# A column for the constant: folding dc into VectorE's head sums in a two-layer linear-attention kernel

## The chip, the core and the metric

The kernel runs on one core of a Trainium2 chip. The metric is the device time of one execution in microseconds (us). Before the change the median of three runs is 866.07 us (866.04 to 866.49).

## The reference

The program is two identical layers, each of a linear-attention block and a GELU block, on x of 2048 rows by 448 columns in float32. With 16 heads of 28 columns the attention is:

```python
phi = lambda t: jnp.where(t > 0, t + 1, jnp.exp(t)) + 1e-6
pq, pk = phi(q), phi(k)                       # q, k, v = layernorm(x) @ wqkv
kv = einsum("bhsd,bhse->bhde", pk, v)
z = einsum("bhsd->bhd", pk)                   # sum of pk over all rows
num = einsum("bhqd,bhde->bhqe", pq, kv)
den = einsum("bhqd,bhd->bhq", pq, z)[..., None] + 1e-6
x = x + (num / den) @ wo
x = x + gelu(layernorm(x) @ w1 + b1) @ w2 + b2
```

The change concerns `den` alone. The kernel keeps e, which is phi without its 1e-6, so that den = sum over d of (e + 1e-6) z_d + 1e-6 = sum of e z_d, plus a constant per head, dc = 1e-6 times the sum of z_d, plus 1e-6.

## The kernel before, in words

The 2048 rows are 16 tiles of 128 rows, and four tiles make a block. A layer has two halves.

- **First half** (`phase1`): for each tile the layer norm, the projections to k and q, phi, and the product G of x with phi(k), summed over all tiles in four PSUM banks. Each float32 factor is split into a high and a low part, and three products stand for one. The phi(q) tiles are stored to DRAM.
- **Second half**: for each block, q over den times a matrix M (kv and wo folded together), the sum with x, a layer norm, and the GELU block `mlp1`, `mlp2`.

Between the halves lies a stretch of some 35 us in each layer, whose order is written out by hand in the table `ORDER` (L660 to L664). It is read token by token, and each engine's instructions stand in the order in which the tokens issue them. The tokens that the change and the prediction speak of are:

- `G`: the last tile's share of G on TensorE (L651). In the middle of it `trans_z` (L794) sums phi(k) over the partitions with a product with ones; ScalarE copies that to zb (L799), and VectorE sums zb by heads into dc (L802, a tile of 128x16).
- `gt`: G's four banks are copied to SBUF as gt, three by ScalarE (L809) and the fourth by VectorE (L811). Behind the first copy ScalarE turns dc into 1e-6 times dc plus 1e-6 (L814).
- `qz1 qz0 qz2 qz3`: for the four tiles of block 0 GpSimd multiplies phi(q) (the tile pq) by zb into the tile pz (`q_z`, L875).
- `qd0`: `q_den` for tile 0: VectorE sums pz by heads into dn (L880), adds dc (L881) and takes the reciprocal rd (L883). `qt0` multiplies pq by rd (L890). `qs1`, `qs2`, `qs3` are both for the other tiles.
- `Qx`, `Qu`, `Qy`: parts of a q projection put in as work for TensorE. `Qp`: phi of an earlier projection, three instructions on ScalarE (L631 to L633), a sum on GpSimd (L634) and a store.
- `kv`: TensorE makes kvp from gt and wv (L821, 32 instructions). `mask`: VectorE masks it into kvm (L825). `m0` to `m3`: TensorE multiplies kvm by wo (L831). `ms0` to `ms3`: ScalarE and VectorE split that into Mh (L843) and Ml (L844).
- `tq1`, `tq0`, `tq2`, `tq3`: TensorE transposes the scaled pq (L901). `qh`, `ql`: ScalarE and VectorE split the result (L908, L913). `o`: TensorE's product with M (L922 to L924). `la`, `lb`, `tu`, `st`, `sp`, `x`: layer norm, a turn through DRAM, and the splits (L347, L348) from which `mlp1` (L997) starts.

The tile pool hands out buffers in turn: a new tile waits until its buffer's last user is done. Before, pz of block 0 lay in three buffers, W5 for tiles 1 and 3, W4 for tile 0, and one of the two `xn` buffers for tile 2. `xn` also holds weights under way in layer 0 and later the normalised rows xm.

Of the kernel before, what the change touches and what calls it, by code (L numbers as in the profile page):

```python
# [11 lines left out]
AF = mybir.ActivationFunctionType  # L12
OP = mybir.AluOpType
# [9 lines left out]
def linear_attn_mlp_kernel(  # L23
# [12 lines left out]
    pe, act, dve, pool, sp = nc.tensor, nc.scalar, nc.vector, nc.gpsimd, nc.sync  # L36
    x0 = x_in[0]
    y_out = out[0]
    S, D = x0.shape
    F = w1.shape[1]  # L40
    H, DH = 16, 28
# [3 lines left out]
    G = 112  # L45
# [21 lines left out]
    def t448(tag, bufs, name, dt=F32):  # L67
        bufs = NH if tag == "H" else bufs
        return work.tile([128, D], dt, name=name, tag=tag, bufs=bufs)
# [3 lines left out]
    def t512(tag, bufs, name, dt=F32, at=0):  # L73
        n = 576 if tag in "BF" else 512
        return work.tile([128, n], dt, name=name, tag=tag, bufs=bufs)[:, at:at + 512]

    def f(ap):
        return ap.bitcast(F32)
# [100 lines left out]
    tiny = consts.tile([128, 1], F32, name="tiny")  # L179
# [3 lines left out]
    mask = consts.tile([G, G], F32, name="mask")  # L183
# [246 lines left out]
    def background(n, m=NF):  # L430

        for g in bg_wait[:m]:
            bg_wait.pop(0)()
        for _ in range(n):
            g = next(bg, None)
            if g is not None:
                bg_wait.append(g)
# [157 lines left out]
    def phi_min():  # L595
        l, t, o = qo.pop(0)
        e = t512("e" if t < NT - 2 else "E", 3 if t < NT - 2 else 2, "eq")[:, :D]
        dve.tensor_scalar(e, o, 0.0, None, op0=OP.min)
        begun.append((l, t, o, e))
# [37 lines left out]
    def stage_g(l, t, acc, mid=lambda: None):  # L637
# [20 lines left out]


    ORDER = [  # L660
# [3 lines left out]
    ] * LAYERS  # L664
# [139 lines left out]
    def trans_gt(tr, acc):  # L804
        tr.gt = []
        for c in range(4):
            s = t512("A" if c < 2 else "B", 2, "gt")[:, :D]
            if c < 3:
                act.copy(s, acc[c])  # L809
            else:  # L810
                dve.tensor_copy(s, acc[c])  # L811
            tr.gt.append(s)
            if c == 0:
                act.activation(tr.dc, tr.dc, AF.Identity, scale=1e-6, bias=tiny)  # L814

    def trans_kv(tr):
        tr.kvp = bank("m", 2, "kvp")[:G, :D]
# [16 lines left out]
    def trans_ms(tr, g):  # L834
        if g == 0:
            tr.Mh, tr.Ml = [], []
        if g % 2 == 0:
            for n in ("Mh", "Ml")[:1 if g else 2]:
                s = work.tile([128, 1024], F32R, name=n, tag="S", bufs=5)
                getattr(tr, n).extend(s[:G, i * D:(i + 1) * D] for i in range(2))  # L840
        if g >= 2:
            tr.Ml.append(t512("F", 2, "Ml", F32R)[:G, :D])
        act.copy(tr.Mh[g], tr.mp[g])  # L843
        dve.tensor_sub(tr.Ml[g], tr.mp[g], f(tr.Mh[g]))  # L844
# [20 lines left out]
    pqt, qs, pzs = {}, {}, {}  # L865

    def load_pq(l, b, j):
        t = b * 4 + j
        pqt[l, t] = t448(f"W{j}", 1, f"pq{l}_{t}")
        sp.dma_start(pqt[l, t], pq_d[l][t * 128:(t + 1) * 128, :])  # L870

    def q_z(l, b, j, tr):
        pz = t512("xn", 2, "pz")[:, :D] if (b, j) == (0, 2) else t448(f"W{4 if b else 4 + j % 2}", 1, "pz")
        pzs[l, b, j] = pz
        pool.tensor_tensor(pz, pqt[l, b * 4 + j], tr.zb, op=OP.mult)  # L875

    def q_den(l, b, j, tr):
        pz = pzs.pop((l, b, j))
        dn = consts.tile([128, H], F32, name="dn", tag="dn", bufs=1)
        dve.tensor_reduce(dn, pz.rearrange("p (h d) -> p h d", d=DH), axis=mybir.AxisListType.X, op=OP.add)  # L880
        dve.tensor_tensor(dn, dn, tr.dc, op=OP.add)  # L881
        rds[l, b, j] = work.tile([128, H], F32, name="rd", tag="rd", bufs=2)
        dve.reciprocal(rds[l, b, j], dn)  # L883

# [2 lines left out]
    def q_times(l, b, j):  # L887
        pq = pqt[l, b * 4 + j]
        p3 = pq.rearrange("p (h d) -> p h d", d=DH)
        dve.scalar_tensor_tensor(p3, p3, 1e-6, rds.pop((l, b, j))[:, :, None].to_broadcast([128, H, DH]),  # L890
                                 op0=OP.add, op1=OP.mult)

    def q_scale(l, b, j, tr):
        q_den(l, b, j, tr)
        q_times(l, b, j)
# [245 lines left out]
    for l in range(LAYERS):  # L1141
        tr = SimpleNamespace(mp={})
        za, acc = phase1(l, tr)
        if l == 0:
            background(0)
        fill = list(range(DEFER, NT))

        def biases(j):
            if l == 0:
                sp.dma_start(b1s, b1.rearrange("(c p) -> p c", p=128))  # L1150
                sp.dma_start(b2b, b2[None, :].to_broadcast([128, D]))

        def pre(j):
            for k in range(4):
                load_pq(l, 1, k)
            if l == 0:
                background(2)

        tok_ = SimpleNamespace(
            Q=lambda j: stage_q(l, fill.pop(0)), Qp=lambda j: fill_qphi(), Qv=lambda j: stage_qphi(j or 9),  # L1160
            Qi=lambda j: phi_first(), Qm=lambda j: phi_min(), Qe=lambda j: phi_exp(), Qj=lambda j: phi_last(), Qs=lambda j: store_phi(),
            Qx=lambda j: stage_q(l, fill[0], (0, 1)), Qu=lambda j: stage_q(l, fill[0], (2,)), Qy=lambda j: stage_q(l, fill.pop(0), (3,)),
            Qa=lambda j: stage_q(l, fill.pop(0), tag="acc"), G=lambda j: stage_g(l, NT - 1, acc, lambda: trans_z(tr, zs[l])),
            ld=lambda j: (load_pq(l, 0, j), load_x(l, j)), gt=lambda j: trans_gt(tr, acc),
            kv=lambda j: trans_kv(tr), mask=lambda j: trans_mask(tr), m=lambda j: trans_m(tr, j),
            ms=lambda j: trans_ms(tr, j), qz=lambda j: q_z(l, 0, j, tr), qs=lambda j: q_scale(l, 0, j, tr),
            qd=lambda j: q_den(l, 0, j, tr), qt=lambda j: q_times(l, 0, j),
            tq=lambda j: q_transpose(l, 0, j), qh=lambda j: q_high(l, 0, j), ql=lambda j: q_low(l, 0, j), o=lambda j: o_mm(l, 0, j, tr),
            la=lambda j: o_ln(l, 0, j), lb=lambda j: o_n(l, 0, j), x=lambda j: m_part(l, 0, j), tu=lambda j: turn_xm(l, j),
            st=lambda j: store_sq(("m", l, 0), j), sp=lambda j: spread(("m", l, 0), j),  # L1170
            sa=lambda j: spread(("m", l, 0), j, (sp, act)), pre=pre, b=biases)
        for tok in ORDER[l].split():
            name, j = tok.rstrip("0123456789"), int("0" + tok.lstrip("abcdefghijklmnopqrstuvwxyzQTG"))
            getattr(tok_, name)(j)
        assert not fill and not qo
        table(AF.Gelu_apprx_tanh)
        q_z(l, 1, 0, tr)
        mlp1(l, 0, 0)
        trans_chunks(tr)
        for b in range(NB):  # L1180
            acc = [bank("acc", 4, f"y{j}")[:, :D] for j in range(4)]
            nxt = b + 1 < NB
            if not nxt and l + 1 < LAYERS:
                st_k = stage_square(wqkv[:, D:2 * D])
                st_q = stage_square(wqkv[:, :D])
                load_to(l + 1, PRE - 1)
            for i in range(NF):
                if i + 1 < NF:
                    mlp1(l, b, i + 1)
                elif nxt:  # L1190
                    mlp1(l, b + 1, 0)
                if l == 0 and b == 0 and i:
                    background(1, 1)
                if i == NF - 2 and not nxt and l + 1 < LAYERS:
                    table(AF.Exp)
                if 9 <= i < 13:
                    add_bias(l, b, i - 9)
                if nxt:
                    behind(l, b, i, tr)
                elif l + 1 < LAYERS:  # L1200
                    if i == 2:
                        split_kq("k", st_k)
                    if i == 5:
                        split_kq("q", st_q)
                    if i in (3, 4, 6, 7, 8):
                        t = (3, 4, 6, 7, 8).index(i)
                        stage_a(l + 1, t)
                        stage_n(l + 1, t)
                        stage_t(l + 1, t)
                        if t % 2:  # L1210
                            stage_sp(l + 1, t)
                    if 9 <= i < 13:
                        stage_x(l + 1, i - 9)
                mlp2(l, b, i, acc)
# [28 lines left out]
```

## Time and profile before

| | |
|---|---|
| median of three runs | 866.07 us (866.04 to 866.49) |
| the profiled execution's own time | 865.61 us |
| its span in the trace | 863.5 us, 2.1 us less |
| TensorE's matmuls busy | 858.1 us, 99% of the span |
| VectorE / ScalarE / GpSimd busy | 495.4 / 350.5 / 210.3 us |
| the stretch between the halves, from the copy zb to the first mlp1 | layer 0: 101.4 to 134.1 us; layer 1: 526.0 to 559.2 us |

Times inside the trace are microseconds from the span's start. A row of the timeline gives the start, the duration, the engine (PE is TensorE's matmuls, PEld its weight loads, DVE is VectorE, ACT is ScalarE, POOL is GpSimd), the line, the operation, what it writes and reads, how many alike were merged, and in brackets the idle time of the engine before it and what ended that. An instruction that waits for a shared resource after its start shows a longer duration, not idle time.

### The profile page before, as it was taken

What the parts mean: (1) busy time and instruction counts of PE and PEld (TensorE: products, weight loads), DVE (VectorE), ACT (ScalarE), POOL (GpSimd) and SP (SyncE); (2) the same over time, 40 slices, a digit from 0 to 9 for tenths busy, and PEclk for the clock granted to TensorE, in tenths of its full rate; (3) what the DMA queues carried; (4) which work ended last, traced back from release to release, by engine and by line L of the source; (5) the groups of instructions that cost most, each with busy time, mean ns of one, the idle gap of its engine ahead of it and who ended that gap; (6) DMA issues with size and microseconds to landing.
All of it is one profiled execution on the core that took longest, in us unless ns stands there. A gap on an engine that the chain in (4) does not pass through costs nothing.

```text
span 863.5 us, 11706 instructions
## 1 busy us (share of the span) xinstructions
PE 858.1 (99%) x4157; PEld 768.4 (89%) x4157; DVE 495.4 (57%) x970; ACT 350.5 (41%) x624; POOL 210.3 (24%) x242
## 2 busy tenths in 40 slices
PE   9999999999999999999999999999999999999998
PEld 8999988888888888888899998988888888888887
DVE  7888686559456443236477877764664383533112
ACT  7676655323323322333356565533232233233231
POOL 3576612235013012012222343120320140140000
PEclk9999999999999999999999999999999999999999
DMA  5485646633313402051145442462332423111001
GB/s 171 152 275 171 207 109 214 194 113 123 120 64 123 137 1 98 1 182 49 49 156 186 160 129 96 143 206 82 121 112 81 140 74 110 49 50 43 1 1 43
DMA packets 68681, 97.89 MB, mean 113 GB/s; under 512 B 9488, under 2 KB 62864, under 8 KB 68624
## 3 DMA queue, kind: packets, MB, share of 16 engines
q1 hardware_dynamic: 67872, 96.76, 34.8%
q8 instruction: 32, 0.52, 0.3%
q10 hardware_dynamic: 752, 0.41, 0.2%
q14 instruction: 25, 0.20, 0.1%
HBM read 57.74 MB, written 36.18 MB: 109 GB/s over the span
## 4 chain that ended last, share of the span: by engine, by line
PE 98%; DVE 1%; issue 0%; ACT 0%; DVEq 0%
PE hp L997 32%; PE y L1027 10%; PE y L1026 10%; PE y L1028 10%; PE G L651 8%; PE psk L365 8%; PE psq L365 7%; PE op L934 2%; PE op L933 2%; PE op L935 2%; PE op L923 1%; PE op L922 1%; PE op L924 1%; PE mp L831 1%; PE op L937 1%; PE psk L579 1%
## 5 line engine op out<-in xcount | busy, mean ns | idle before, releaser
L1003 DVE TENSOR_TENSOR gl<-g,gh 128x512 fp32r<-128x512 f32 x112 | 83.2, 743 | 292.2 <-ACT gh L1002 292.2
L999 ACT ACTIVATE g<-hp,b1s 128x512 f32<-128x512 f32 x112 | 77.2, 689 | 400.6 <-PE hp L997 400.6
L1027 PE MATMUL y<-w2l,gh 128*128 128x448 f32 x447 | 163.6, 366 | 0.0
L1026 PE MATMUL y<-w2h,gh 128*128 128x448 f32 x447 | 162.0, 362 | 0.0
L1028 PE MATMUL y<-w2h,gl 128*128 128x448 f32 x447 | 160.0, 358 | 0.0
L997 PE MATMUL hp<-XH,w1h 128*128 128x512 f32 x336 | 130.7, 389 | 0.0
L997 PE MATMUL hp<-XH,w1l 128*128 128x512 f32 x336 | 130.7, 389 | 0.0
L997 PE MATMUL hp<-XL,w1h 128*128 128x512 f32 x336 | 130.1, 389 | 0.0
L215 POOL TENSOR_TENSOR brs<-bve,mhalf 128x1 f32<-128x1 f32 x55 | 34.6, 629 | 264.1 <-DVE bve L214 263.7
L1026 PEld LDWEIGHTS y<-w2h,gh 128*128 128x128 f32 x447 | 83.7, 187 | 9.4
L1027 PEld LDWEIGHTS y<-w2l,gh 128*128 128x128 f32 x447 | 83.9, 188 | 7.0
L1028 PEld LDWEIGHTS y<-w2h,gl 128*128 128x128 f32 x447 | 84.0, 188 | 5.0
L997 PEld LDWEIGHTS hp<-XL,w1h 128*128 128x128 f32 x336 | 63.1, 188 | 13.1
L997 PEld LDWEIGHTS hp<-XH,w1h 128*128 128x128 f32 x336 | 63.0, 187 | 10.7
L997 PEld LDWEIGHTS hp<-XH,w1l 128*128 128x128 f32 x336 | 63.1, 188 | 9.9
L1002 ACT CAST gh<-g 128x512 fp32r<-128x512 f32 x112 | 69.5, 621 | 3.6
L365 PE MATMUL psk<-wk,XH 128*128 128x448 f32 x210 | 61.8, 364 | 0.0
L875 POOL TENSOR_TENSOR pz<-pq,zb 128x448 f32<-128x448 f32 x32 | 37.4, 1176 | 96.4 <-DVE dn L880 62.1
L365 PE MATMUL psq<-wq,XH 128*128 128x448 f32 x196 | 57.1, 365 | 0.0
L490 POOL TENSOR_TENSOR xnl<-x,xnh 128x384 fp32r<-128x384 f32 x32 | 35.1, 1097 | 68.3 <-ACT xnh L489 55.0
L348 DVE TENSOR_TENSOR XL<-sp,XH 128x512 fp32r<-128x512 f32 x58 | 46.8, 818 | 5.5 <-ACT XH L347 5.5
L651 PE MATMUL G<-kh,xnh 128*128 128x448 f32 x128 | 46.7, 367 | 0.0
(185 smaller groups left out, 1490.9 us busy)
## 6 DMA issues: line engine op xcount, KB each, us to landing
x<-in_A_x_dram SPq DMA_DIRECT2D x32, 224.0 KB, 4.0
pq_d<-eq SPq DMA_DIRECT2D x32, 224.0 KB, 2.5
pq<-pq_d SPq DMA_DIRECT2D x32, 224.0 KB, 3.5
x<-x_d SPq DMA_DIRECT2D x32, 224.0 KB, 3.8
sq_a<-sq SPq DMA_DIRECT2D x13, 512.0 KB, 2.9
sp<-sq_a SPq DMA_DIRECT2D x52, 128.0 KB, 3.0
sq_q<-sq SPq DMA_DIRECT2D x12, 512.0 KB, 2.7
sp<-sq_q SPq DMA_DIRECT2D x48, 128.0 KB, 2.8
```

Source lines behind the costliest of these rows:

```text
L348: eng.tensor_tensor(lo.rearrange("p (c i n) -> p c i n", c=4, n=32), x, f(h), op=OP.subtract)
L365: pe.matmul(o, x, p, start=(i == 0), stop=(i == 10))
L490: pool.tensor_tensor(lo[:, :TL], xn[:, :TL], f(h[:, :TL]), op=OP.subtract)
L651: pe.matmul(acc[c], w, k, start=first and c not in others[0], stop=last and c not in others[1])
L875: pool.tensor_tensor(pz, pqt[l, b * 4 + j], tr.zb, op=OP.mult)
L997: pe.matmul(o, w, r, start=(k == 0), stop=(k == len(made) - 1))
L999: act.activation(g, hp, AF.Gelu_apprx_tanh, bias=b1s[:, i:i + 1])
L1002: act.copy(gh, g)
L1003: dve.tensor_sub(gl, g, f(gh))
L1026: pe.matmul(acc[j], gh[:, s], w2h[:, i], start=first, stop=False)
L1027: pe.matmul(acc[j], gh[:, s], w2l[:, i], start=False, stop=False)
L1028: pe.matmul(acc[j], gl[:, s], w2h[:, i], start=False, stop=stop)
```

## The change

pz of block 0 becomes a tile of 16 heads by 29 columns, 464 wide, always in one of the two `xn` buffers. GpSimd writes the products into columns 0 to 27 of each head (new L874). A new helper `times_tiny` has ScalarE write 1e-6 times dc plus 1e-6 into column 28 (new L882, token `dz`), and VectorE's sum runs over 29 columns (new L889), so that the add of dc disappears for block 0. Blocks 1 to 3 keep the add; for them the token `dc` turns dc as before, but later. In the order, the products of tiles 2 and 3 move behind `qs1` and `qd0`.

```diff
-  "Q ld1 ld0 ld2 ld3 G qz1 qz0 qz2 qz3 gt qs1 Qx Qp kv qd0 tq1 Qu mask qt0 qh1 ql1 m0 tq0 qs2 b ms0 qh0 m1 ms1 m2 "
+  "Q ld1 ld0 ld2 ld3 G qz1 qz0 gt dz1 dz0 qs1 qz2 dz2 Qx Qp kv qd0 qz3 dz3 dc tq1 Qu mask qt0 qh1 ql1 m0 tq0 qs2 b ms0 qh0 m1 ms1 m2 "
...
-            if c == 0:
-                act.activation(tr.dc, tr.dc, AF.Identity, scale=1e-6, bias=tiny)
...
-        pz = t512("xn", 2, "pz")[:, :D] if (b, j) == (0, 2) else t448(f"W{4 if b else 4 + j % 2}", 1, "pz")
-        pzs[l, b, j] = pz
-        pool.tensor_tensor(pz, pqt[l, b * 4 + j], tr.zb, op=OP.mult)
+        pq = pqt[l, b * 4 + j]
+        if b == 0:
+            pz = pzs[l, b, j] = t512("xn", 2, "pz")[:, :H * (DH + 1)].rearrange("p (h d) -> p h d", d=DH + 1)
+            pool.tensor_tensor(pz[:, :, :DH], pq.rearrange("p (h d) -> p h d", d=DH),
+                               tr.zb.rearrange("p (h d) -> p h d", d=DH), op=OP.mult)
+            return
+        pz = pzs[l, b, j] = t448("W4", 1, "pz")
+        pool.tensor_tensor(pz, pq, tr.zb, op=OP.mult)
+
+    def times_tiny(out, ds):
+
+        act.activation(out, ds, AF.Identity, scale=1e-6, bias=tiny)
...
-        dve.tensor_reduce(dn, pz.rearrange("p (h d) -> p h d", d=DH), axis=mybir.AxisListType.X, op=OP.add)
-        dve.tensor_tensor(dn, dn, tr.dc, op=OP.add)
+        if b:
+            pz = pz.rearrange("p (h d) -> p h d", d=DH)
+        dve.tensor_reduce(dn, pz, axis=mybir.AxisListType.X, op=OP.add)
+        if b:
+            dve.tensor_tensor(dn, dn, tr.dc, op=OP.add)
...
+            dz=lambda j: times_tiny(pzs[l, 0, j][:, :, DH], tr.dc), dc=lambda j: times_tiny(tr.dc, tr.dc),
```

VectorE's row in layer 0 from the fourth copy of G to the mask is shown first, before the change; dn is a tile's head sums, rd its reciprocal, and pq0_1, pq0_0 are the phi(q) of tiles 1 and 0.

```order
L811 COPY gt_1375<-G3_335 128x448
L880 TENSOR_REDUCE dn_1377<-pz_1360 128x16
L881 TENSOR_TENSOR dn_1377<-dn_1377,dc_1350 128x16
L883 RECIPROCAL rd_1380<-dn_1377 128x16
L890 SCALAR_TENSOR_TENSOR pq0_1_1326<-pq0_1_1326,rd_1380 128x448
L880 TENSOR_REDUCE dn_1414<-pz_1362 128x16
L881 TENSOR_TENSOR dn_1414<-dn_1414,dc_1350 128x16
L883 RECIPROCAL rd_1417<-dn_1414 128x16
L825 TENSOR_TENSOR kvm_1427<-kvp_1397,mask_121 112x448
L890 SCALAR_TENSOR_TENSOR pq0_0_1330<-pq0_0_1330,rd_1417 128x448
```

The same place of VectorE's row with the change:

```order
L811 COPY gt_1370<-G3_335 128x448
L889 TENSOR_REDUCE dn_1374<-pz_1360 128x16
L893 RECIPROCAL rd_1376<-dn_1374 128x16
L900 SCALAR_TENSOR_TENSOR pq0_1_1326<-pq0_1_1326,rd_1376 128x448
L889 TENSOR_REDUCE dn_1413<-pz_1362 128x16
L893 RECIPROCAL rd_1415<-dn_1413 128x16
L823 TENSOR_TENSOR kvm_1429<-kvp_1396,mask_121 112x448
L900 SCALAR_TENSOR_TENSOR pq0_0_1330<-pq0_0_1330,rd_1415 128x448
```

Two adds are gone ahead of the mask; two more go behind it, in front of the reciprocals of tiles 2 and 3.

ScalarE's row from the copy zb to the last instruction of `Qp`, before:

```order
L799 ACTIVATE zb_1348<-zp_1345,zc_119 128x448
L809 COPY gt_1368<-G0_332 128x448
L814 ACTIVATE dc_1350<-dc_1350,tiny_117 128x16
L809 COPY gt_1371<-G1_333 128x448
L809 COPY gt_1373<-G2_334 128x448
L631 ACTIVATE eq_1390<-psq_1314 128x448
L632 ACTIVATE ep_1391<-psq_1314 128x448
L633 ACTIVATE eq_1390<-eq_1390 128x448
```

And with the change, down to the split of tile 1:

```order
L799 ACTIVATE zb_1348<-zp_1345,zc_119 128x448
L809 COPY gt_1364<-G0_332 128x448
L809 COPY gt_1366<-G1_333 128x448
L809 COPY gt_1368<-G2_334 128x448
L882 ACTIVATE pz_1360<-dc_1350,tiny_117 128x16
L882 ACTIVATE pz_1362<-dc_1350,tiny_117 128x16
L882 ACTIVATE pz_1379<-dc_1350,tiny_117 128x16
L631 ACTIVATE eq_1389<-psq_1314 128x448
L632 ACTIVATE ep_1390<-psq_1314 128x448
L633 ACTIVATE eq_1389<-eq_1389 128x448
L882 ACTIVATE pz_1417<-dc_1350,tiny_117 128x16
L882 ACTIVATE dc_1350<-dc_1350,tiny_117 128x16
```

The copies of G's second and third bank have lost the instruction on dc ahead of them, and three writes of 128x16 stand ahead of `Qp`. The third, into pz_1379 (tile 2), lies in the buffer of pz_1360 (tile 1), so it waits for VectorE's sum of tile 1.

GpSimd's row, before:

```order
L875 TENSOR_TENSOR pz_1360<-pq0_1_1326,zb_1348 128x448
L875 TENSOR_TENSOR pz_1362<-pq0_0_1330,zb_1348 128x448
L875 TENSOR_TENSOR pz_1364<-pq0_2_1334,zb_1348 128x448
L875 TENSOR_TENSOR pz_1366<-pq0_3_1338,zb_1348 128x448
L634 TENSOR_TENSOR eq_1390<-ep_1391,eq_1390 128x448
```

And with the change:

```order
L874 TENSOR_TENSOR pz_1360<-pq0_1_1326,zb_1348 128x16x28
L874 TENSOR_TENSOR pz_1362<-pq0_0_1330,zb_1348 128x16x28
L874 TENSOR_TENSOR pz_1379<-pq0_2_1334,zb_1348 128x16x28
L634 TENSOR_TENSOR eq_1389<-ep_1390,eq_1389 128x448
L874 TENSOR_TENSOR pz_1417<-pq0_3_1338,zb_1348 128x16x28
```

The product of tile 3 has moved behind the sum of `Qp`, and waits for VectorE's sum of tile 0, whose buffer it takes. TensorE's and SyncE's rows are the same in both, apart from line numbers.

## The prediction

> **What bounds the kernel now.** I read the busy times first, then what TensorE waited for, then the timeline of the two stretches between the halves.
>
> ```profile
> PE 858.1 (99%) x4157; PEld 768.4 (89%) x4157; DVE 495.4 (57%) x970; ACT 350.5 (41%) x624; POOL 210.3 (24%) x242
> ```
>
> TensorE is the bound, and the change leaves its instructions alone. All that an edit elsewhere can win is TensorE's waiting. The view of waits has it complete:
>
> ```profile
> PE warm L170 <- DVE one L164: 1.1, 1, 1.1
> PE mp L831 <- DVE kvm L825: 0.5, 1, 0.5
> PE psk L579 <- ACT wk L137: 0.2, 1, 0.2
> ```
>
> Three waits, 1.8 us in all; two are in the launch, out of the change's reach. The one within it is of `m0` for the mask kvm. So nothing in the trace lets this change win more than about 0.7 us, and faster by 0.2% (1.7 us of 866.07; about what a measurement of this kernel can tell from no change) is out of reach. What it can lose has no such lid. The wait is in layer 1, and the timeline there (matmuls, VectorE, ScalarE, GpSimd) shows how it comes about:
>
> ```profile
> 526.25 0.37 PE L651 MATMUL G<-kh,xnl 128*128 128x448 f32 x1
> 526.57 0.53 ACT L809 COPY gt<-G 128x448 f32<-128x448 f32 x1
> 526.75 4.46 POOL L875 TENSOR_TENSOR pz<-pq,zb 128x448 f32<-128x448 f32 x4 [6.24 <-ACT zb L799]
> 526.86 0.36 PE L651 MATMUL G<-kh,xnl 128*128 128x448 f32 x1
> ...
> 527.36 0.31 ACT L814 ACTIVATE dc<-dc,tiny 128x16 f32<-128x16 f32 x1 [0.26 <-DVE dc L802]
> 527.71 0.97 ACT L809 COPY gt<-G 128x448 f32<-128x448 f32 x2
> ...
> 528.27 0.61 DVE L880 TENSOR_REDUCE dn<-pz 128x16 f32<-128x448 f32 x1
> 528.56 0.56 ACT L631 ACTIVATE eq<-psq 128x448 f32<-128x448 f32 x1
> 528.68 3.31 PE L821 MATMUL kvp<-gt,stg 128*112 128x112 f32 x32
> 528.98 1.17 DVE L881 TENSOR_TENSOR dn<-dn,dc 128x16 f32<-128x16 f32 x1
> 529.42 0.60 ACT L633 ACTIVATE eq<-eq 128x448 f32<-128x448 f32 x1
> 530.19 0.25 DVE L883 RECIPROCAL rd<-dn 128x16 f32<-128x16 f32 x1
> 530.47 1.22 DVE L890 SCALAR_TENSOR_TENSOR pq<-pq,rd 128x448 f32<-128x448 f32 x1
> 531.18 1.52 POOL L634 TENSOR_TENSOR eq<-ep,eq 128x448 f32<-128x448 f32 x1
> 531.62 0.61 DVE L880 TENSOR_REDUCE dn<-pz 128x16 f32<-128x448 f32 x1
> 532.26 0.47 DVE L881 TENSOR_TENSOR dn<-dn,dc 128x16 f32<-128x16 f32 x1
> 532.67 0.36 PE L372 MATMUL psq<-wq,XL 128*128 128x448 f32 x1
> 532.93 0.56 DVE L825 TENSOR_TENSOR kvm<-kvp,mask 112x448 f32<-112x448 f32 x1
> 533.41 0.61 DVE L890 SCALAR_TENSOR_TENSOR pq<-pq,rd 128x448 f32<-128x448 f32 x1
> 533.55 1.00 PE L831 MATMUL mp<-wot,kvm 112*112 112x448 f32 x2 [0.51 <-DVE kvm L825]
> 534.39 0.60 PE L901 MATMUL tq<-ident,pq 128*112 128x128 f32 x4
> ```
>
> kvp is done at 531.99, but VectorE reaches the mask only at 532.93. What holds it up are operations with two operands in SBUF that last as long as GpSimd works: the add takes 1.17 and 0.47 us, and the product with rd 1.22, where the same product takes 0.61 once GpSimd is idle. They end where a GpSimd instruction ends (four products from 526.75, 1.1 apiece, so one ends near 530.1, as does the first add). One side has the port, and the other stands still until it lets go. The sums (0.61) and the reciprocal (0.25) never stretch. Layer 0 has the same order with a luckier phase:
>
> ```profile
> 103.73 0.62 DVE L880 TENSOR_REDUCE dn<-pz 128x16 f32<-128x448 f32 x1
> ...
> 107.34 1.14 POOL L634 TENSOR_TENSOR eq<-ep,eq 128x448 f32<-128x448 f32 x1
> 107.61 0.56 DVE L825 TENSOR_TENSOR kvm<-kvp,mask 112x448 f32<-112x448 f32 x1
> ...
> 108.09 0.87 DVE L890 SCALAR_TENSOR_TENSOR pq<-pq,rd 128x448 f32<-128x448 f32 x1
> ```
>
> ```profile
> 108.23 0.27 PEld L831 LDWEIGHTS mp<-wot,kvm 112*112 112x112 f32 x2 [0.21 <-DVE kvm L825]
> 109.03 0.40 PEld L901 LDWEIGHTS tq<-ident,pq 128*112 128x112 f32 x4 [0.53 <-issue]
> ```
>
> There the mask is done at 108.17, the loads for `m0` follow at 108.23, and no matmul waits. But the load for `tq0` starts 0.07 after the scaled tile 0 (108.09 + 0.87 = 108.96): layer 0 has no slack at `tq0`.
>
> **The change, part by part.**
>
> *ScalarE before the sum.* The slot of dc (527.36 to 527.71, 0.35) leaves the front, so the second and third copies move up: at least by 0.35, at most to where their banks are ready (526.25 + 0.37 and 526.86 + 0.36, just after the first copy). The third then ends between 527.98 and 528.33 instead of 528.68, and the write for tile 1 (0.31, as dc's row) ends between 528.25 and 528.6. VectorE's sum now waits for it: it starts at 528.27 as before, or up to 0.33 later. I take the early end, since nothing else stands ahead of these copies. The 29th column makes the sum 464 elements instead of 448, 4% of 0.61, 0.02 us.
>
> *The two adds ahead of the mask* go: by their rows 1.17 and 0.47 in layer 1. The time does not fall by 1.64, since they were mostly waiting for GpSimd, and the next operation with two SBUF operands inherits that. So step by step in layer 1: sum of tile 1 to 528.88; reciprocal to about 529.2; GpSimd's product of tile 2, which now waits for that sum, starts at about 528.98, when tile 0's is done, and holds the port to 530.1; the product with rd then ends at about 530.6 (before: 531.69). Sum of tile 0 to 531.2, reciprocal to 531.4. Now kvp is the later one: mask from about 532.1 to 532.66. `m0` can follow the projection at 532.87 (532.67 and 0.20, the step of these matmuls) instead of 533.55: 0.68 earlier. The mask has 0.2 us to spare there, VectorE ahead of it 0.6.
>
> *What is late next: `tq0`.* It needs tile 0 scaled, behind the mask. On ScalarE the write for tile 2 waits for the sum of tile 1, with `Qp` queued behind it: write at 528.93, `Qp` from 529.28, and 1.46 later (528.56 to 530.02 before) it ends at 530.74. GpSimd's sum of `Qp` runs 530.8 to 531.9 and tile 3's product 531.9 to 533.0; VectorE's product for tile 0, issued at 532.6, gets the port at 533.0 and ends at 533.5. `tq0` comes 0.84 behind `m0` (533.55 to 534.39), at 533.71, and is not held up. Layer 1: **-0.68 us**; with the late end of the first item everything from the sum on is 0.33 later, tile 0 is ready at 533.84 and `tq0` goes at 533.95: -0.44.
>
> *The same in layer 0* gives: sum of tile 1 to 104.35, write for tile 2 at 104.4, `Qp` from 104.75 to 106.2, its sum on GpSimd 106.26 to 107.36, tile 3's product to 108.46, VectorE's product for tile 0 half a us behind that (before, GpSimd let go at 108.48 and the product ended at 108.96): 109.0. So `tq0` there stands where it stood, within 0.1; with the late end 0.35 later. Layer 0: **+0.05**, bounds -0.05 and +0.4. The earlier mask wins nothing there, since `tq0` sets the pace.
>
> *Off the path.* Of the adds of tiles 2 and 3 nothing is waited for. The writes for tile 3 and of dc stand on ScalarE between 531.3 and 532.0, where it waits for `tq1` anyway; the next user of dc is block 1. SyncE's queue has the same order: the store of `Qp` leaves its producer about a us earlier, and the biases behind it too.
>
> *GpSimd's products of 16 pieces.* The trace has no such product. Low end: as before, 1.1 us. For the high end two neighbours:
>
> ```profile
> 96.54 1.02 POOL L490 TENSOR_TENSOR xnl<-x,xnh 128x384 fp32r<-128x384 f32 x1
> 97.52 0.31 POOL L491 TENSOR_TENSOR xnh<-x,xnh 128x64 fp32r<-128x64 f32 x1
> ```
>
> 384 and 64 elements cost 1.02 and 0.31: 2.2 ns an element and 0.17 us an instruction (estimate). Were each head paid as an instruction, a product would cost 15 x 0.17 = 2.55 more, 3.6 us. I take 1.1: inputs are contiguous as before and only the write skips one column in 29. GPSIMD Engine Reference of the Trainium skill, § 7 "Performance pitfalls for Q7 kernels", has reads whose step is over 8 bytes at about half as much again per element; were this write, whose step inside a head is 4 bytes, charged so, an estimate of 1.65 a product would make the sum about +0.1 instead of -0.6. No row here shows such a step.
>
> *Does the gain last?* From `tq0` on, TensorE's own products feed the layer norm, the turn through DRAM and the splits, so these move with it:
>
> ```profile
> 557.07 1.20 ACT L347 CAST XH<-sp 128x512 fp32r<-128x512 f32 x2
> ...
> 559.16 0.39 PE L997 MATMUL hp<-XH,w1h 128*128 128x512 f32 x1
> ```
>
> The last high part is there 0.9 us before `mlp1` asks for it, and behind that the waits show none on which a gain could be lost. **Sum: -0.68 + 0.05 = -0.6 us**, bounds -0.75 and 0. On the profiled execution's own 865.61 (863.5 and 2.1 around it) that is 865.0; the runs' median lies 0.46 above it, so the forecast is 866.07 - 0.6 = **865.5**.
>
> **The rivals.**
>
> *The gain is given back at the port.* `tq0` in both layers hangs on who has the port when VectorE asks. With products of 1.2 to 1.9 us, or a sum that starts late, VectorE misses a turn in one layer or the other. Stepping the same chain with 1.2, 1.35, 1.65 and 1.9 a product gives -0.1, 0.0, +0.15 and +0.1 over both layers; a late sum alone 0.0. For it: layer 0 has 0.07 us of slack. Against: in layer 1 there is a wait of 0.68 to give away. Time about 866.1.
>
> *Slower: GpSimd pays for the pieces.* One mechanism: from some product length on, tile 3's product holds the port when VectorE comes to scale tile 2, and VectorE's Ml (L844) behind that is late for `o1`. At twice, 2.2 us: in layer 0 the products of tiles 1 and 0 end at 104.7 and 106.9, the mask ends at about 108.9, tile 0 is scaled at 110.15 (`tq0` +1.2), tile 3's product runs 111.2 to 113.4, tile 2 is scaled at 113.9 and `o1` waits another 0.6: +1.8. In layer 1 likewise +0.7. Together +2.5: 868.6. At 3.6 us it is about +14. The point is between 1.9 and 2.2 a product. For it: no strided write in the trace. Against: inputs contiguous, one instruction. The same page and section of the Trainium skill charges about 102 cycles for each read command that does not overlap the one before it; if the 16 heads were 16 commands, an estimate at that page's 1.2 GHz is 1.36 us more a product, 2.46, and +4.6 us. That is this rival's case; no row here shows it.
>
> *It does not do what it says:* the add's wait is taken over whole by the product behind it, and the mask stays late. Against: the mask can be 0.2 late before `m0` moves at all. 866.1, counted with the first rival.
>
> **How the numbers follow.** The forecast 57%, given back (or no effect) 27%, slower through GpSimd 13%, and 3% for a gain that the waits do not show. The first two are within 0.2%: 0.84 with rounding; slower 0.13; faster 0.03. The range holds the first two with the runs' spread (0.03 below to 0.42 above the median): 864.9 to 866.9.
>
> **What would show it.** In the changed profile: kvm no longer named in TensorE's waits in layer 1; VectorE's two sums and reciprocals without a stretched add; tile 3's product directly behind the sum of `Qp`, and VectorE's product for tile 0 stretched behind it; in layer 1 the step from kvp's end to `tq0` 1.7 us instead of 2.4 (531.99 to 534.39). The forecast is wrong if a product of GpSimd takes over 1.2 us, if `tq0` or `o` shows up among the waits, or if the sum of tile 1 waits for ScalarE.

## The result and the profile after

The changed kernel takes 864.65 us (median of 22 runs, 864.2 to 866.2), and before takes 866.23 us (22 runs, 865.07 to 868.23) in the same series. The ratio is 0.9985, with a 95% interval of 0.9978 to 0.9991, that is 0.8 to 1.9 us less. The difference is inside the 0.2% that the prediction called no change; its sign is the forecast one, and 864.65 lies 0.25 us below the low end of the stated range.

The profiled execution of the changed kernel happens to be one of its longer ones: 866.08 us, a span of 864.1 us, 0.6 more than the span of before. A comparison of the two spans would mislead. Stage by stage the traces say what happened. First, TensorE's busy time and the whole of its waits, after the change:

```profile
PE 859.2 (99%) x4157; PEld 768.3 (89%) x4157; DVE 493.6 (57%) x962; ACT 351.9 (41%) x632; POOL 210.9 (24%) x242
```

```profile
PE warm L170 <- DVE one L164: 1.1, 1, 1.1
PE psk L579 <- ACT wk L137: 0.3, 1, 0.3
```

The wait for the mask is gone; only the launch is left. To measure a stage independently of what came before it, I take two marks: the last matmul of the column sums, zp, and the first transpose of tile 0, `tq0`. The marks that the prediction doesn't show are, in before:

```profile
100.99 0.37 PE L797 MATMUL zp<-zl,ones 128*128 128x448 f32 x1
...
525.63 0.37 PE L797 MATMUL zp<-zl,ones 128*128 128x448 f32 x1
```

With `tq0` at 109.07 and 534.39, before takes 8.08 us in layer 0 and 8.76 in layer 1. The same stretch of layer 1 after the change, with all that TensorE, VectorE, ScalarE and GpSimd do on the path:

```profile
526.87 0.37 PE L797 MATMUL zp<-zl,ones 128*128 128x448 f32 x1
...
527.99 2.27 POOL L874 TENSOR_TENSOR pz<-pq,zb 128x448 f32<-128x448 f32 x2 [6.24 <-ACT zb L799]
528.95 0.97 ACT L809 COPY gt<-G 128x448 f32<-128x448 f32 x2 [0.61 <-PE G L651]
529.80 0.53 ACT L882 ACTIVATE pz<-dc,tiny 128x16 f32<-128x16 f32 x2
529.92 3.31 PE L819 MATMUL kvp<-gt,stg 128*112 128x112 f32 x32
530.24 0.64 DVE L889 TENSOR_REDUCE dn<-pz 128x16 f32<-128x464 f32 x1 [0.65 <-ACT pz L882]
530.95 1.14 POOL L874 TENSOR_TENSOR pz<-pq,zb 128x448 f32<-128x448 f32 x1 [0.69 <-DVE dn L889]
531.19 1.37 DVE L900 SCALAR_TENSOR_TENSOR pq<-pq,rd 128x448 f32<-128x448 f32 x1
532.49 0.62 DVE L889 TENSOR_REDUCE dn<-pz 128x16 f32<-128x464 f32 x1
532.62 1.15 POOL L634 TENSOR_TENSOR eq<-ep,eq 128x448 f32<-128x448 f32 x1 [0.53 <-ACT eq L633]
533.15 0.25 DVE L893 RECIPROCAL rd<-dn 128x16 f32<-128x16 f32 x1
533.32 0.57 DVE L823 TENSOR_TENSOR kvm<-kvp,mask 112x448 f32<-112x448 f32 x1
533.71 1.71 POOL L874 TENSOR_TENSOR pz<-pq,zb 128x448 f32<-128x448 f32 x1
533.81 0.61 DVE L900 SCALAR_TENSOR_TENSOR pq<-pq,rd 128x448 f32<-128x448 f32 x1
534.12 0.92 PE L829 MATMUL mp<-wot,kvm 112*112 112x448 f32 x2
534.87 0.60 PE L911 MATMUL tq<-ident,pq 128*112 128x128 f32 x4
```

From 526.87 to 534.87 are 8.00 us, 0.76 less than before. The mask starts at 533.32, 0.09 behind the end of kvp (529.92 + 3.31) and 0.17 behind the start of the reciprocal. VectorE and kvp are now ready at almost the same time, and TensorE does not wait for the mask. Layer 0 shows the same figures, 101.10 to 109.10, again 8.00:

```profile
101.10 0.37 PE L797 MATMUL zp<-zl,ones 128*128 128x448 f32 x1
...
107.95 1.70 POOL L874 TENSOR_TENSOR pz<-pq,zb 128x448 f32<-128x448 f32 x1
108.03 0.61 DVE L900 SCALAR_TENSOR_TENSOR pq<-pq,rd 128x448 f32<-128x448 f32 x1
...
108.17 0.35 PEld L829 LDWEIGHTS mp<-wot,kvm 112*112 112x112 f32 x2
108.35 0.92 PE L829 MATMUL mp<-wot,kvm 112*112 112x448 f32 x2
...
109.10 0.60 PE L911 MATMUL tq<-ident,pq 128*112 128x128 f32 x4
```

Together the stages give 0.08 + 0.76 = **0.84 us**. Of layer 1's part, 0.67 is that `m0` starts earlier (7.92 us behind zp before, 7.25 after). The other 0.09 lies inside `m0`: its two matmuls now take 0.92 us, where before they took 1.00, in layer 0 too:

```profile
108.24 1.00 PE L831 MATMUL mp<-wot,kvm 112*112 112x448 f32 x2
```

Before, the weight load of `m0` waited for the mask in both layers (in layer 0 it is the load at 108.23, with 0.21 of waiting); after, it does not. In all eleven profiles, of these two kernels and of the experiments below, the pair takes 1.00 or 1.01 where its load waits for kvm, and 0.92 where it doesn't.

Where did this execution lose more than that? In a place that the change doesn't touch, layer 1's first half. The view of stretches for 449 to 499 us, before and then after (behind each engine's busy time, the number of instructions; then the granted clock):

```profile
449.00:499.00 50.00, 50.00 (x252) 46.89 (x251) 41.54 (x94) 29.63 (x54) 16.59 (x27) 1.00 0.54 171
```

```profile
449.00:499.00 50.00, 50.00 (x246) 45.93 (x246) 40.80 (x93) 29.35 (x54) 15.57 (x26) 1.00 0.53 171
```

The same 50 us hold 252 matmuls in the one execution and 246 in the other, at the same granted clock: 6 matmuls at 0.2 us are 1.2 us. With these taken off the span of after is 862.9, and single runs of one and the same kernel differ by steps of about that size. Of all runs reported below one, of experiment 9, took 1755.78 us; its ratio leaves that run out, and its cause is not known.

### The profile page after: what moved, and what is told of

Its sections match the earlier page's. It is cut to its first block, busy times and chain, and to the rows that moved or that the text cites. A ratio compares the mean times of both kernels' runs of the same rounds, so it can differ in the third digit from the quotient of the medians.

```text
span 864.1 us, 11713 instructions
## 1 busy us (share of the span) xinstructions
PE 859.2 (99%) x4157; PEld 768.3 (89%) x4157; DVE 493.6 (57%) x962; ACT 351.9 (41%) x632; POOL 210.9 (24%) x242
## 4 chain that ended last, share of the span: by engine, by line
PE 99%; DVE 0%; issue 0%; ACT 0%; DVEq 0%
PE hp L1007 32%; PE y L1037 10%; PE y L1036 10%; PE y L1038 10%; PE G L651 8%; PE psk L365 8%; PE psq L365 7%; PE op L944 2%; PE op L943 2%; PE op L945 2%; PE op L933 1%; PE op L932 1%; PE op L934 1%; PE kvp L819 1%; PE mp L829 1%; PE op L947 1%
## 5 line engine op out<-in xcount | busy, mean ns | idle before, releaser
L878 POOL TENSOR_TENSOR pz<-pq,zb 128x448 f32<-128x448 f32 x24 | 27.7, 1155 | 90.5 <-DVE dn L889 62.0
```

## The experiments

Nine experiments were run, in three series, each beside before: the two kernels once more, and seven edited ones. The table gives the marks (start of the last zp, start of `tq0`, and their difference), from the timeline of each kernel's profiled execution, the median of its runs, and the ratio to before with its 95% interval.

| kernel | layer 0: zp, tq0, us | layer 1: zp, tq0, us | both, against before | median us | ratio |
|---|---|---|---|---|---|
| before | 100.99, 109.07, 8.08 | 525.63, 534.39, 8.76 | | 866.23 | |
| changed | 101.10, 109.10, 8.00 | 526.87, 534.87, 8.00 | -0.84 | 864.65 | 0.9985 (0.9978 to 0.9991) |
| 1 before again | 100.63, 108.71, 8.08 | 525.57, 534.33, 8.76 | 0.00 | 865.71 | 1.0001 (0.9992 to 1.0009) |
| 2 changed again | 100.60, 108.60, 8.00 | 525.23, 533.23, 8.00 | -0.84 | 864.56 | 0.9988 (0.9979 to 0.9997) |
| 3 no adds | 101.18, 109.28, 8.10 | 526.38, 534.39, 8.01 | -0.73 | 865.33 | 0.9989 (0.9980 to 0.9998) |
| 4 adds back | 101.01, 109.60, 8.59 | 526.35, 534.94, 8.59 | +0.34 | 866.20 | 1.0001 (0.9992 to 1.0010) |
| 5 no add, tile 1 | 101.75, 109.85, 8.10 | 526.42, 534.42, 8.00 | -0.74 | 865.11 | 0.9989 (0.9979 to 0.9998) |
| 6 no add, tile 0 | 101.44, 109.51, 8.07 | 527.25, 535.49, 8.24 | -0.53 | 865.52 | 0.9997 (0.9988 to 1.0007) |
| 7 order alone | 100.96, 109.04, 8.08 | 526.91, 535.68, 8.77 | +0.01 | 866.01 | 0.9999 (0.9990 to 1.0008) |
| 8 column early | 100.94, 109.05, 8.11 | 525.77, 533.78, 8.01 | -0.72 | 864.60 | 0.9986 (0.9977 to 0.9996) |
| 9 products twice | 100.94, 109.81, 8.87 | 526.37, 534.83, 8.46 | +0.49 | 866.19 | 1.0002 (0.9992 to 1.0012) |

The marks of both kernels repeat to 0.01 us in the second execution that was profiled, while whole runs scatter by over 1 us. So the verdicts below rest on the marks, and the times only say that nothing else of that size happened.

### 1 and 2: both kernels again

No edit. What was expected of before:

> The kernel before, unchanged, timed against itself. Theory A (the change is worth the 0.83 us that the two traces show between the halves, and the rest of the 1.6 us between the medians is scatter of the runs): a ratio of 1.000 whose spread is some tenths of a us, and single runs about 1 us apart. Theory B (the whole 1.6 us is the change's): medians that repeat within 0.2 us and no steps of 1 us between runs.

and of the changed kernel:

> The changed kernel, unchanged, timed once more. Theory A: 0.8 to 0.9 us below before where the fastest runs of both are compared, and a span of 862.5 to 863.2 us in the profile unless the trace shows a slow window like the one from 448 to 499 us of the first profile. Theory B: 1.6 us below, also between the fastest runs.

Before against itself comes out at 1.0001, with an interval of 0.8 us to either side, and its runs lie from 865.19 to 867.44: theory A as to scatter. The changed kernel's span is 862.5 in this profile, against 863.6 of before's. At the lower quarter of the runs (864.27 and, over the series' 33 runs of before, 865.47) the difference is 1.2 us, and at the medians 1.35 (864.56 and 865.91). That is more than theory A's 0.8 to 0.9 and less than theory B's 1.6. Matmul by matmul, the two profiles part by 0.16 in layer 0's stretch (half of it up to `tq0`) and 0.77 in layer 1's; 0.14 more appears at the layer boundary, near 447.7 us, where the program is the same. So of the difference of the medians 0.8 to 0.9 us stands in the traces as the change's. What is known of the rest stands under "The medians beyond the marks" below.

### 3: the adds left out, nothing else

```diff
-        dve.tensor_tensor(dn, dn, tr.dc, op=OP.add)
+        if b:
+            dve.tensor_tensor(dn, dn, tr.dc, op=OP.add)
```

> The kernel before, with block 0's four adds of dc left out (the constant is missing from den there) and nothing else moved. Theory A (the two adds ahead of the mask are the cause, the column and the new order only the means): the wait of 0.5 us for the mask in layer 1 is gone, and the time from the copy zb to tq0 there falls from 8.35 to 7.6 us; in all -0.7 to -0.85 us against before. Rival (the gain comes from the new order of GpSimd's row, or from dc leaving ScalarE's front): the wait stays, or half of it, and the time is within 0.3 us of before.

Layer 1 falls from 8.76 to 8.01, and the wait for the mask is gone. In its timeline the mask now waits for kvp, with VectorE idle ahead of it:

```profile
532.78 0.62 DVE L825 TENSOR_TENSOR kvm<-kvp,mask 112x448 f32<-112x448 f32 x1 [0.61 <-PE kvp L821]
```

Layer 0 does not gain (8.10), because there the sum of `Qp` and the product for tile 0 still meet at the port, and `tq0` waits for the product:

```profile
107.55 1.14 POOL L634 TENSOR_TENSOR eq<-ep,eq 128x448 f32<-128x448 f32 x1
...
108.12 1.05 DVE L891 SCALAR_TENSOR_TENSOR pq<-pq,rd 128x448 f32<-128x448 f32 x1
```

So the adds are the cause of the gain in layer 1, 0.75 of 0.76, and neither the column nor the order is needed for it. Layer 0's 0.08 does not come from leaving out the adds alone.

### 4: the changed kernel with the adds back

```diff
-        if b:
-            dve.tensor_tensor(dn, dn, tr.dc, op=OP.add)
+        dve.tensor_tensor(dn, dn, tr.dc, op=OP.add)
```

> The changed kernel with the add put back behind each sum of 29 columns (den then gets a constant that it should not). Theory A: the add of tile 0 asks for the port while GpSimd runs the sum of Qp and is held until that ends, some 0.6 us, in both layers; the mask and tq0 come about 0.8 us later in each, so +1.5 us against the changed kernel, +0.7 against before. Rival (order and copies carry the gain): within 0.3 us of the changed kernel.

Each layer loses 0.59 (8.00 to 8.59), 1.18 together against the expected 1.5, and 0.34 more than before takes. The mechanism is the expected one: tile 0's add stands still while GpSimd runs the sum of `Qp` (0.64 instead of the 0.18 that tile 1's takes here), and the mask is late again.

```profile
532.10 1.14 POOL L634 TENSOR_TENSOR eq<-ep,eq 128x448 f32<-128x448 f32 x1 [0.53 <-ACT eq L633]
...
532.63 0.64 DVE L890 TENSOR_TENSOR dn<-dn,dc 128x16 f32<-128x16 f32 x1
...
534.10 1.01 PE L829 MATMUL mp<-wot,kvm 112*112 112x448 f32 x2 [0.34 <-DVE kvm L823]
```

With the adds, the new kernel is 0.51 slower than before in layer 0 and 0.17 faster in layer 1. In layer 0 the sum of tile 1 starts 0.63 later behind zp than before (3.37 and 2.74), and the late chain then meets the sum of `Qp`. That the late column is the reason was not tested apart.

### 5 and 6: one add at a time

```diff
-        dve.tensor_tensor(dn, dn, tr.dc, op=OP.add)
+        if (b, j) != (0, 1):     # 6: (0, 0)
+            dve.tensor_tensor(dn, dn, tr.dc, op=OP.add)
```

For tile 1:

> The kernel before without the add of tile 1 alone (the first one ahead of the mask, 1.17 us in layer 1; den of tile 1 lacks its constant). Times here run from the start of the last matmul of the column sums zp to the first transpose tq0, 8.08 us in layer 0 and 8.76 in layer 1 of before. Theory A: the product with rd takes the add's place at the port and ends half a us behind GpSimd's third product, the rest of the chain fits ahead of kvp's end, and layer 1 gains all of it: 8.0 to 8.1 in both layers, -0.7 us in all. Rival (each add costs what its row shows, and only both together are enough): still 8.2 to 8.4 in layer 1.

For tile 0:

> The kernel before without the add of tile 0 alone (the second one ahead of the mask, 0.47 us in layer 1; den of tile 0 lacks its constant). Theory A: tile 1's add still waits out GpSimd's third product and its product the fourth, so the sum of tile 0 stays at 5.99 us behind zp, and the reciprocal and the mask follow at once: the mask some 0.45 us earlier, tq0 at 8.3 to 8.4 in layer 1, 8.1 in layer 0; -0.4 us in all. Rival (whichever add goes, the port wait moves on to the next operation and the mask stays): 8.7 in layer 1, nothing gained.

Without tile 1's add alone layer 1 gains all of its 0.76 (8.00). Without tile 0's alone it gains 0.52 (8.24, expected 8.3 to 8.4). The two do not add up: 0.76 + 0.52 is more than the 0.75 of both. With tile 1's add still there, it waits out a product of GpSimd, and the mask follows the reciprocal as soon as it can:

```profile
530.60 1.16 DVE L882 TENSOR_TENSOR dn<-dn,dc 128x16 f32<-128x16 f32 x1
531.79 0.25 DVE L884 RECIPROCAL rd<-dn 128x16 f32<-128x16 f32 x1
532.07 1.22 DVE L891 SCALAR_TENSOR_TENSOR pq<-pq,rd 128x448 f32<-128x448 f32 x1
533.22 0.61 DVE L880 TENSOR_REDUCE dn<-pz 128x16 f32<-128x448 f32 x1
533.86 0.25 DVE L884 RECIPROCAL rd<-dn 128x16 f32<-128x16 f32 x1
534.03 0.56 DVE L825 TENSOR_TENSOR kvm<-kvp,mask 112x448 f32<-112x448 f32 x1
```

What an add is worth is thus not its row but the turns at the port that it brings about, up to the time at which kvp is ready.

### 7: the order alone

```diff
-  "Q ld1 ld0 ld2 ld3 G qz1 qz0 qz2 qz3 gt qs1 Qx Qp kv qd0 tq1 ..."
+  "Q ld1 ld0 ld2 ld3 G qz1 qz0 gt qs1 qz2 Qx Qp kv qd0 qz3 tq1 ..."
```

> The kernel before with the new order of GpSimd's row alone: the products of tiles 2 and 3 behind qs1 and qd0, no column, adds and buffers as before. Theory A: the adds wait for whatever GpSimd runs, and that the sum of Qp now stands third changes nothing for them: tq0 at 8.1 and 8.7 to 8.8 as before, no difference in time. Rival (the order carries the gain): 8.0 in both layers, -0.8 us.

8.08 and 8.77, with the old wait in the view of waits, unchanged:

```profile
PE mp L831 <- DVE kvm L825: 0.5, 1, 0.5
```

The new order by itself moves nothing.

### 8: the column of tile 1 early

```diff
             tr.gt.append(s)
+            if c == 0:
+                times_tiny(pzs[tr.l, 0, 1][:, :, DH], tr.dc)
...
-  "... gt dz1 dz0 qs1 ..."
+  "... gt dz0 qs1 ..."
```

> The changed kernel with the write for tile 1's column in the slot that dc had, behind the first copy of G, so that VectorE's sum of tile 1 starts with GpSimd's product, some 0.7 us earlier, as the prediction had assumed. Theory A: the mask still waits for kvp, nothing is gained, and the port now stands as the prediction's steps had it (tile 3's product takes it before VectorE asks for tile 0): tq0 at 8.0 to 8.15 in both layers, up to 0.2 us slower than the changed kernel. Rival (in the changed kernel the late sum holds up the mask, which has no slack): tq0 at 7.9, 0.1 to 0.2 us faster.

8.11 and 8.01. Nothing is gained by an earlier sum, and in layer 0 `tq0` comes 0.11 later than in the changed kernel. In layer 1 the mask waits for kvp; the product for tile 0 behind it meets tile 3's product and is held a little:

```profile
531.87 1.14 POOL L876 TENSOR_TENSOR pz<-pq,zb 128x448 f32<-128x448 f32 x1
...
532.17 0.62 DVE L825 TENSOR_TENSOR kvm<-kvp,mask 112x448 f32<-112x448 f32 x1 [0.60 <-PE kvp L821]
...
532.71 0.78 DVE L902 SCALAR_TENSOR_TENSOR pq<-pq,rd 128x448 f32<-128x448 f32 x1
```

In layer 0 it is held longer, and that is what `tq0` waits for:

```profile
107.32 1.14 POOL L876 TENSOR_TENSOR pz<-pq,zb 128x448 f32<-128x448 f32 x1
...
107.88 1.07 DVE L902 SCALAR_TENSOR_TENSOR pq<-pq,rd 128x448 f32<-128x448 f32 x1
```

This kernel runs the prediction's steps nearly as they were written: it had forecast `tq0` 8.13 us behind zp in layer 0 (8.08 + 0.05) and 8.08 in layer 1, and VectorE ready 0.6 ahead of the mask, which is the 0.60 of idle time above.

### 9: the products made twice

```diff
+            for _ in range(2):
-            pool.tensor_tensor(pz[:, :, :DH], ...
+                pool.tensor_tensor(pz[:, :, :DH], ...
```

> The changed kernel with each of GpSimd's four products of block 0 made twice, one behind the other, to see what longer products would cost (the rival of the prediction that ended slower; 2.2 us a tile in two instructions). Times from the last matmul of zp to tq0, 8.00 us in both layers of the changed kernel. Theory A (the chain over the port): tile 0's sum comes about 1.1 us later, so does the mask, and the product for tile 0 then waits for a turn of the port: mp 0.8 later, tq0 at 9.1 to 9.4 in both layers, +2.2 to +2.8 us against the changed kernel and +1.4 to +2.0 against before. Rival (GpSimd is off the path, idle time covers the longer products): 8.0 to 8.2 and no difference to the changed kernel.

8.87 and 8.46, +1.33 us against the changed kernel: the direction of theory A, at about half its size. The mask is late in both layers, 0.62 and 0.21 us as TensorE sees it:

```profile
108.97 1.00 PE L829 MATMUL mp<-wot,kvm 112*112 112x448 f32 x2 [0.62 <-DVE kvm L823]
```

```profile
533.98 1.01 PE L829 MATMUL mp<-wot,kvm 112*112 112x448 f32 x2 [0.21 <-DVE kvm L823]
```

The product for tile 0 takes 0.61 in both layers, though GpSimd has work all the while; the expectation had it wait. GpSimd's row of six products lasts 7.96 us, 1.1 more than six of 1.14, so here it was GpSimd that stood still while VectorE worked. The prediction's slower rival had priced 2.2 us a product at +2.5 against before; as two instructions they cost +0.49. What one instruction of that length would cost was not tried.

## Why the prediction was right, and where not

- **What bounds the kernel, and the most it could win:** right. The one wait in reach is gone, and `m0` comes 0.67 earlier in layer 1, against 0.68 forecast.
- **The two adds ahead of the mask:** right in kind. That 1.64 us of rows would yield less than half of that, because kvp takes over as the last to come, is shown by experiments 3, 5 and 6.
- **ScalarE before the sum:** wrong. The prediction let G's second and third copies move up by 0.35 to 0.7. They did not move: they start 0.09 us behind G's last product (528.49 and 0.37), as they did before (527.71, behind 527.62), and dc ahead of them had stood in a gap. So the writes of the column came behind the copies' full length, and the sum of tile 1 began 3.37 us behind zp instead of 2.64, 0.73 later; the late end that the prediction allowed for was 0.33. The row shows the wait for ScalarE (0.65) that the prediction names as a sign of being wrong.
- **That this did no harm:** luck. By the prediction's own steps a sum only 0.33 late gives the gain back, -0.44 in layer 1 and +0.4 in layer 0. The sum was later than that, and the gain stayed whole, because the turns at the port fell another way (next point but one). Experiment 8, with the sum early, is 0.12 slower than the changed kernel, not faster.
- **The slack ahead of the mask:** said to be 0.6 us for VectorE, in fact about none, since the sum was late.
- **What is late next, `tq0`:** right that the product for tile 0 and tile 3's product of GpSimd are rivals for the port there; wrong in who comes first. In the changed kernel the sum of `Qp` ends late enough that both ask at nearly the same time (GpSimd at 533.71, VectorE at 533.81; 107.95 and 108.03 in layer 0). VectorE's product takes its bare 0.61, and GpSimd's stretches to 1.71 and 1.70. GpSimd's rows start first, and why VectorE gets the port all the same no run shows. This stretch, and not the 16 pieces, is why one product of GpSimd takes over 1.2 us, another of the prediction's signs. With the earlier sum of experiment 8 the order is the forecast one.
- **Layer 0:** forecast +0.05, measured -0.08, out of the bounds of -0.05 and +0.4 by 0.03. Two things had held `tq0` there, each to about 8.08 us behind zp, and the prediction saw one. The product for tile 0 ended only 7.97 us behind zp; and the load of `m0` waited 0.21 for the mask, which made `m0`'s pair 0.08 longer. "No matmul waits" was right by the view of waits, but the earlier mask did have something to win. In the changed kernel both are early. In experiment 6 the mask alone is early, the product ends at 7.97 as before, and `tq0` comes at 8.07.
- **Does the gain last:** right. From the last zp to the first `mlp1` are 32.94 us in layer 0 (100.99 to 133.93; the 134.1 of the table is too late) and 33.53 in layer 1 before, 32.85 and 32.86 after; in the profiles of experiments 1 and 2, 32.94 and 33.62 before, 32.78 and 32.85 after.
- **GpSimd's products of 16 pieces:** right. Two take 2.27 and one 1.14, as the contiguous ones did. The surcharge that the Trainium skill has in GPSIMD Engine Reference, § 7 "Performance pitfalls for Q7 kernels", for reads with steps over 8 bytes, does not show in this write. No product here reads with such a step, so the surcharge itself was not tried.
- **The size:** the terms give -0.6, the marks -0.84, and the medians -1.58 with an interval of -0.8 to -1.9. The forecast time was 0.85 above the measured one. Of this 0.24 is in the terms: `m0`'s shorter pair, 0.09 and 0.08, which the prediction put at nothing, layer 0's 0.05 that did not come, and rounding.
- **The medians beyond the marks:** part lies outside the span, where the prediction kept 2.1 us. A run's time less its span is at least 2.03 in every run of before whose span is on record, and in experiments 1 and 7; in the changed kernel and all the other experiments, the slower ones too, it goes down to between 1.67 and 1.76, and its median to between 1.7 and 2.0. So 0.1 to 0.3 us of the difference does not lie between the halves; its cause is open. The median spans are 862.8 and 862.6 for the changed kernel and, in the experiments' series, 863.7 and 863.8 for before, 0.9 to 1.2 apart. What is left is of the size by which the medians of before differ from series to series (865.91 to 866.23).

## What to carry to other kernels

In this kernel a short VectorE operation with two operands in SBUF could cost the rest of what GpSimd was doing when it was issued: the add takes 0.18 us undisturbed (experiment 4) and took 0.47, 0.64 and 1.17. Most of such a row is waiting time, which passes to the next such operation when the first is removed. Price it by stepping the chain up to the next fixed time (here the end of kvp), not by adding up rows. And before letting instructions move up into a freed slot, look at what they were waiting for: here the slot had lain in a gap. A view that shows no waiting matmul can still hide a late weight load: here it made a pair of matmuls 0.08 us longer.

## What was not expected of the hardware

In three of the eleven profiled executions TensorE steps some 2% slower for 50 us, at a granted clock that reads 1.00 throughout: 246 matmuls instead of 252, 203 ns apiece instead of 198. The stretch lies between 449 and 499 us in the profiles of the changed kernel and of experiments 6 and 7 and not in those of the others, so kernels with and without the change have it; experiment 7's:

```profile
449.00:499.00 50.00, 50.00 (x247) 45.92 (x246) 40.81 (x93) 29.40 (x54) 15.54 (x26) 1.00 0.53 172
```

Each costs 1.0 to 1.2 us (5 or 6 matmuls of 0.2), more than the change is worth. Its cause was not looked for.
